# First unit's queries kept on the chip, and its maxima put ahead of the second block's keys

## The chip, the cores and the metric

One of the eight cores of one Trainium2 chip runs the kernel. The metric is the time of one execution in microseconds (us); the median of several runs is given. The engines named below are PE (TensorE, matrix products; PEld its weight loads), DVE (VectorE), ACT (ScalarE), POOL (GpSimd) and SP (SyncE, which issues most transfers).

## What is computed

A transformer block with modulated layer norms. There are 2048 rows of 512 numbers, 32 query heads of 16 numbers, and one key and value head that all of them share.

```python
mod = (silu(c) @ w_mod).reshape(1, 6, 1, -1)
sa, ca, ga, sb, cb, gb = (mod[:, i] for i in range(6))
h = layernorm(x) * (1 + ca) + sa
q = (h @ wq).reshape(1, 2048, 32, 16).transpose(0, 2, 1, 3)
k, v = h @ wk, h @ wv
p = softmax(einsum("bhqd,bkd->bhqk", q, k) * 16 ** -0.5)
o = einsum("bhqk,bkd->bhqd", p, v)
x = x + ga * (o.transpose(0, 2, 1, 3).reshape(1, 2048, 512) @ wo)
h = layernorm(x) * (1 + cb) + sb
x = x + gb * (gelu(h @ w1 + b1) @ w2 + b2)
```

## The kernel before

**Numbers in two parts.** Products run on rounded float32 (F32R). Each operand is split into a high part, which is the rounded number, and a low part, which is what the rounding left. A product of two such operands is three products summed in PSUM: high by high, low by high, high by low (`mm3`, with `split` to make the parts).

**Units.** The queries are cut into blocks of 256 rows, and each of those into 8 groups of 4 heads. One group of one block is a unit, 64 in all. A unit's queries lie in one of four buffers `qst` of 128 partitions. The partitions form two halves, s = 0 and s = 1, for the even and the odd pairs of heads. In each half, 16 rows hold the low part of the queries, 32 rows hold the high part twice, and rows 48 and 49 hold the unit's maxima (high and low part). The rows of `ks` that stand against them hold the keys' high part, high part, low part and -1. So one product of 64 rows gives the scores, and with the maxima in place it gives the scores less their maximum.

**Two passes over the keys.** For each unit the kernel first needs the maximum of every row of scores. `Max.step` issues one *max product* `m` (128 queries by 512 keys, line L517) on PE and one reduction `mx` on DVE (L522). The products use three PSUM banks, so the fourth product waits for the first reduction. When all 32 of a unit are done, `put_max` reduces once more, turns the result, and sends it by four small transfers into rows 48 and 49. Then `sexp` computes the score products `e` (L597), ACT takes the exponentials `p` (L598), and `pv` sums `acc` from them (L609). In the main loop, the e, p and acc of one unit run beside the max products of units further on and beside projections and the MLP, in an order that is fixed when the program is written.

**The prologue.** The change lies in the stretch before the main loop. Blocks there are 512 rows of `x`, four of them (0 to 3). For each block b: `stats1(b)` takes the row statistics on DVE; `xhat1(b)` normalises four tiles; `heads(b)` turns each of four column groups on PE (`turn1`, tiles `tp`) and applies the modulation (`mod1`, which makes the two parts of `h`); `keys(b)` sums keys and values (`kps`, 12 products in four steps) and `kv_out` copies them into `ks`; `low_k(b)` makes the keys' low part in half 0, and `repeat_k(b)` copies it into half 1.

Queries come from `qproj(b, g)`: 12 products sum the four pairs of heads of group g into one PSUM bank. The two parts are then sent to a tensor `dq` in DRAM (`send_q`), and `load_q(u)` fetches the rows of unit u back in the layout of `qst`: two transfers for each half, s = 1 first. Group 0 of block 0 serves units 0 and 1, group 1 serves unit 2.

All five engines run their instructions strictly in the order written (`manual_schedule`). `SLOTS` writes out the order of the last part of the prologue by hand. Each slot is a number of `Max.step`s, which alternate between the halves, followed by steps of other work named in the slot. `FIRST_MAX` is the order of the first 64 max products: pairs of unit and key block, eight products for each pair, four in each half. The key block `kc` needs `keys(kc)`, `low_k(kc)` and `repeat_k(kc)`. Before the main loop starts, 56 max products are issued: 54 in the slots and two in a loop behind them.

Ahead of the slots the order is: group 0 of block 0 is projected and sent while `stats1(2)` runs, and `load_q(0)` and `load_q(1)` follow; then `keys(0)`, `low_k(0)`, all of `heads(1)`, `stats1(3)`, `repeat_k(0)`, and `xhat1` of blocks 2 and 3 on ACT. The first slot has four max products and two steps of `keys 1`.

`prep_w2` belongs to the main loop. It loads 11 pieces of `w2`, multiplies them by a modulation row and splits them, on POOL; the last piece has 96 rows, and its tile is cleared first.

Of the kernel before, what the change touches and what calls it, by code (L numbers as in the profile page):

```python
# [14 lines left out]
P = 128  # L15
# [6 lines left out]
LEAD = 6  # L22
LEAD_0 = 6
FIRST_MAX = ((0, 0), (1, 0), (0, 1), (1, 1), (0, 2), (0, 3), (1, 2), (1, 3))
SLOTS = ((4, "keys 1", "keys 1"), (2, "keys 1", "keys 1"), (2, "low 1", "heads 2"), (2, "heads 2", "k 1"), (2, "heads 2"), (2, "heads 2", "v 0"),
# [4 lines left out]
MAX_WAIT = (1, 4)  # L30
# [17 lines left out]
def raw(ap):  # L48
    return ap.bitcast(F32)
# [3 lines left out]
def adaln_mqa_mlp(  # L53
# [76 lines left out]
    def split(dst_h, dst_l, src, eng_h, eng_l, between=None):  # L130
        if eng_h is nc.gpsimd:
            eng_h.tensor_scalar(out=dst_h, in0=src, scalar1=1.0, scalar2=0.0, op0=ALU.mult, op1=ALU.add)
        elif eng_h is nc.scalar:
            eng_h.copy(dst_h, src)
        else:
            eng_h.tensor_copy(out=dst_h, in_=src)
        if between:
            between()
        eng_l.tensor_tensor(out=dst_l, in0=src, in1=raw(dst_h), op=ALU.subtract)
# [188 lines left out]
    def prep_wq(g):  # L328
        gs = slice(g * P, (g + 1) * P)
        for j in range(2):  # L330
# [3 lines left out]
            nc.scalar.copy(dh, src)  # L334
            nc.gpsimd.tensor_tensor(out=dl, in0=src, in1=raw(dh), op=ALU.subtract)

    hts = {}
    hts_stats = {}
    pad(att, 64, "pad5")
# [13 lines left out]
            nc.gpsimd.tensor_scalar(out=nm, in0=nm, scalar1=-1.0, scalar2=0.0, op0=ALU.mult, op1=ALU.add)  # L353
        hts_stats[b] = mv, rs, nm

    def xhat1(b, eng):

        mv, rs, nm = hts_stats[b]
        xt = xts[b]
        for t in range(QT):  # L360
            if eng is nc.scalar:
                nc.scalar.activation(xt[:, t, :], xt[:, t, :], AF.Identity, scale=rs[:, t:t + 1], bias=nm[:, t:t + 1])
            else:
                eng.tensor_scalar(out=xt[:, t, :], in0=xt[:, t, :], scalar1=mv[:, t, 0:1], scalar2=rs[:, t:t + 1],
                                  op0=ALU.subtract, op1=ALU.mult)
            yield
# [15 lines left out]
    def kv_products(b):  # L382
        hH, hL = hts[b]
        kps[b] = psum.tile([P, BQ], F32, name=f"kps{b}", tag="x" if b == 3 else "v")
        return mm3(kps[b], [(wkH[:, k, :], wkL[:, k, :], hH[:, k, :], hL[:, k, :]) for k in range(KD)], 3)

    def kv_out(b):
        ps = kps[b]
        cols = slice(b * BQ, (b + 1) * BQ)
        vt = pro.tile([P, BQ], F32, name=f"vt{b}", tag="vt", bufs=2)  # L390
        for r in range(2):
            nc.scalar.copy(ks[64 * r:64 * r + 48, cols], ps[64 * r:64 * r + 48, :])
        nc.scalar.copy(vt[32:64, :], ps[32:64, :])
        vts[b] = vt

    def low_k(b):
        cols = slice(b * BQ, (b + 1) * BQ)
        nc.vector.tensor_tensor(out=ks[32:48, cols], in0=kps.pop(b)[32:48, :], in1=raw(ks[32:48, cols]), op=ALU.subtract)

    def repeat_k(b):  # L400
        cols = slice(b * BQ, (b + 1) * BQ)
# [727 lines left out]
    def prep_w2():  # L1129
        rp = wts_pool["rest"]  # L1130
        wfs = {}

        def load(f):
            fw = min(P, F - f * P)
            wf = wfs[f] = rp.tile([P, D], F32, name=f"w2f{f}", tag="wf", bufs=3)
            if fw < P:
                nc.gpsimd.memset(wf, 0.0)
            nc.sync.dma_start(out=wf[:fw], in_=w2[f * P:f * P + fw, :])

        def work(f):  # L1140
            g = f // KD
            if f % KD == 0:
                w2s.append([att.tile([P, min(KD, NF - f), D], F32R, name=f"w2{p_}{g}", tag=f"big{g + 1}{p_}") for p_ in "HL"])
            nc.gpsimd.tensor_tensor(out=wfs[f], in0=wfs[f], in1=gb, op=ALU.mult)
            split(w2s[g][0][:, f % KD, :], w2s[g][1][:, f % KD, :], wfs[f], nc.gpsimd, nc.gpsimd)

        for i, _ in enumerate(prepare(NF, load, work)):
            yield
            while i >= 1 and i - 1 < NF and not sent.issuperset(((i - 1) // KD + 1, g) for g in range(KD)):
                yield  # L1150
# [70 lines left out]
    def run(job, n=99):  # L1221
        for _ in range(n):
            if next(job, True):
                return
# [23 lines left out]
    def q_group():  # L1248
        for i in range(KD):
            next(projections[0])  # L1250
            if i == KD - 1:
                next(projections.pop(0))
            yield
# [5 lines left out]
    stats1(0)  # L1259
    run(xhat1(0, dve))  # L1260
    prep_wkv()
    prep_wq(0)
    for k in range(KD):
        mod_rows(psr, k, wms[k])
# [9 lines left out]
    load_constants()  # L1274
    mod1(0, 2, act, dve)
    mod1(0, 3, act, dve)
    rows = xhat1(1, act)
    run(rows, 2)

    def first_q(t):  # L1280
        if t == 1:
            run(q_group())
            load_q(0)
            load_q(1)

    stats1(2, first_q)
    run(rows)
    run(keys(0))
    low_k(0)
    load_mods(0)  # L1290
    load_mods(1)
    h1 = heads(1)
    run(h1, 2)

    def last_h(t):
        if t == QT - 1:
            run(h1)

    stats1(3, last_h)
    load_mods(2)  # L1300
    repeat_k(0)
    run(xhat1(2, act))
    run(xhat1(3, act))
    work = {"keys 1": keys(1), "heads 2": heads(2), "heads 3": heads(3), "q 1": q_group(), "keys 2": keys(2), "keys 3": keys(3),
# [198 lines left out]
```

## Time and profile before

| | us |
|---|---|
| median of 3 runs | 1586.05 |
| lowest and highest of them | 1585.31, 1586.48 |
| the profiled execution | 1589.15 |
| its span, first to last instruction | 1587.3 |

| engine | busy us | share of the span |
|---|---|---|
| PE | 1562.7 | 98% |
| DVE | 1406.0 | 89% |
| ACT | 1204.3 | 76% |
| POOL | 692.8 | 44% |

The profile is of one execution. An engine's share is a mean over stages with different limits, so it says little about one stage. A row of the timeline gives the start, the length, the engine, the line, the operation, the tiles written and read, the shape and the count. Brackets at its end hold how long the engine had been idle and what the profile takes to have ended the wait. Where a wait is for several things, the name is that of the one that came last by the profile's reckoning; if that had long been done, it was another, often a transfer. PEclk is the granted share of PE's full clock; the mean over the span is 0.992.

### The profile page before, as it was taken

The page shows a single profiled execution, that of the slowest core. Times are in us where ns is not written, and L with a number is a line of the kernel's source. Part 1 is how long each engine was busy: PE and PEld are TensorE (multiplying, and loading weights), DVE is VectorE, ACT ScalarE, POOL GpSimd, SP SyncE. Part 2 cuts the span into 40 slices and gives each one's busy share as a digit, 9 for nine tenths or more (in the row PEclk, how much of TensorE's full clock was granted, in tenths as well). Part 3 has the DMA queues.
Part 4 walks back from the last instruction along what each step waited for, and adds up shares of the span by engine and source line. Part 5 has one row for each costly group of instructions (what it writes and reads, how often), then busy time and mean ns, then how long its engine had stood idle before and what let it go on. Part 6 is the DMA issues. An engine that isn't in the chain of part 4 may idle for free.

```text
span 1587.3 us, 43409 instructions
## 1 busy us (share of the span) xinstructions
PE 1562.7 (98%) x17491; PEld 1043.9 (66%) x17491; DVE 1406.0 (89%) x2491; ACT 1204.3 (76%) x2417; POOL 692.8 (44%) x1242
## 2 busy tenths in 40 slices
PE   5999999999999999999999999999999999999999
PEld 3556655567766676666766676666766677676667
DVE  6889999899999998999999999999999999999715
ACT  5477777778877887778877887778877788778853
POOL 4345447446513472345622464334712465324721
PEclk8899999999999999999999999999999999999999
DMA  7135423312012120212112130212112130121231
GB/s 263 67 108 177 141 70 101 100 33 97 32 56 67 56 86 23 90 35 94 46 40 86 44 99 19 70 54 86 56 32 92 35 108 22 60 72 50 94 139 68
DMA packets 81022, 121.74 MB, mean 77 GB/s; under 512 B 15966, under 2 KB 55646, under 8 KB 80564
## 3 DMA queue, kind: packets, MB, share of 16 engines
q1 hardware_dynamic: 80804, 118.95, 22.6%
q8 instruction: 137, 2.24, 0.6%
q14 instruction: 65, 0.53, 0.1%
q10 hardware_dynamic: 16, 0.00, 0.0%
HBM read 91.13 MB, written 27.27 MB: 75 GB/s over the span
## 4 chain that ended last, share of the span: by engine, by line
PE 94%; ACT 3%; DVE 1%; DMA 1%; issue 0%; SPq 0%; POOL 0%; DVEq 0%; ACTq 0%
PE acc L609 32%; PE e L597 19%; PE m L517 19%; PE w1ps L193 8%; PE w2ps L193 6%; PE wops L193 3%; PE qps L193 2%; ACT p L598 2%; PE w2ps L187 2%; PE w1ps L187 1%; DVE mx L522 1%; PE tp L193 1%; PE kps L164 1%; PE tp L371 0%; PE modr L289 0%; DMA wm<-in_w_mod_dram 0%
## 5 line engine op out<-in xcount | busy, mean ns | idle before, releaser
L522 DVE TENSOR_REDUCE mx<-m 128x1 f32<-128x512 f32 x2048 | 1271.6, 681 | 105.6 <-PE m L517 95.6
L598 ACT ACTIVATE p<-e 128x512 f32<-128x512 f32 x2048 | 1066.6, 601 | 290.5 <-PE e L597 198.9
L517 PE MATMUL m<-ks,qst 64*128 64x512 f32 x2048 | 829.4, 433 | 6.4 <-DVE ve L205 4.9
L597 PE MATMUL e<-qst,ks 64*128 64x512 f32 x2048 | 729.5, 411 | 2.0 <-ACT wqH L334 1.3
L609 PE MATMUL acc<-p,va 128*32 128x256 f32 x8192 | 550.2, 385 | 1.7 <-DMA qst<-dq 1.7
L517 PEld LDWEIGHTS m<-ks,qst 64*128 64x128 f32 x2048 | 367.4, 184 | 104.6 <-DVE mx L522 85.7
L597 PEld LDWEIGHTS e<-qst,ks 64*128 64x128 f32 x2048 | 356.9, 184 | 112.6 <-ACT p L598 102.6
L609 PEld LDWEIGHTS acc<-p,va 128*32 128x32 f32 x8192 | 214.6, 109 | 219.6 <-issue 113.3
L193 PE MATMUL w1ps<-h2H,w1t 64*128 64x256 f32 x1232 | 236.6, 288 | 0.0
L193 PEld LDWEIGHTS w1ps<-h2H,w1t 64*128 64x128 f32 x1232 | 184.0, 185 | 31.7 <-issue 22.2
L566 POOL TENSOR_SCALAR mt<-turned 8x32 f32<-8x32 f32 x256 | 53.5, 209 | 342.7 <-DVE turned L572 330.6
L193 PE MATMUL w1ps<-h2L,w1t 64*128 64x256 f32 x616 | 169.5, 275 | 0.0
L193 PE MATMUL w2ps<-w2H,gH 64*128 64x256 f32 (+1 forms) x546 | 161.0, 295 | 0.0
L193 PE MATMUL w2ps<-w2H,gL 64*128 64x256 f32 (+1 forms) x546 | 153.9, 282 | 0.0
L193 PE MATMUL w2ps<-w2L,gH 64*128 64x256 f32 (+1 forms) x546 | 153.4, 281 | 0.0
L193 PEld LDWEIGHTS w1ps<-h2L,w1t 64*128 64x128 f32 x616 | 113.7, 185 | 0.0
L193 PEld LDWEIGHTS w2ps<-w2H,gH 64*128 64x128 f32 x546 | 100.5, 184 | 11.7 <-issue 5.4
L193 PEld LDWEIGHTS w2ps<-w2H,gL 64*128 64x128 f32 x546 | 100.7, 184 | 1.7
L193 PEld LDWEIGHTS w2ps<-w2L,gH 64*128 64x128 f32 x546 | 100.7, 184 | 1.3
L949 POOL TENSOR_SCALAR tt<-tt 128x256 f32<-128x256 f32 x77 | 31.2, 406 | 143.8 <-ACT tt L948 143.8
L193 PE MATMUL wops<-woH,onH 64*128 64x256 f32 x224 | 67.9, 303 | 0.0
L193 PE MATMUL wops<-woL,onH 64*128 64x256 f32 x224 | 62.2, 278 | 0.0
(220 smaller groups left out, 1613.1 us busy)
## 6 DMA issues: line engine op xcount, KB each, us to landing
w1t<-dw SPq DMA_DIRECT2D x82, 512.0 KB
qst<-dq SPq DMA_DIRECT2D x128, 64.0 KB
do<-oc SPq DMA_DIRECT2D x64, 128.0 KB
dw<-w1s SPq DMA_DIRECT2D x11, 512.0 KB
xt<-in_A_x_dram SPq DMA_DIRECT2D x4, 1024.0 KB
dq<-qH SPq DMA_DIRECT2D x16, 256.0 KB
dq<-qL SPq DMA_DIRECT2D x16, 256.0 KB
qst<-dq SPq DMA_DIRECT2D x128, 32.0 KB
```

Source lines behind the costliest of these rows:

```text
L164: nc.tensor.matmul(ps, a, b_, start=begin and n == 0, stop=end and n == last)
L187: nc.tensor.matmul(ps, a, b_, start=first_, stop=last_)
L193: nc.tensor.matmul(ps, a[rows], b_[rows], start=first_ and s == 0, stop=last_ and s == 1)
L517: nc.tensor.matmul(m, qsts[u][rows, j, t * P:(t + 1) * P], ks[rows, kc * 512:(kc + 1) * 512], start=True, stop=True)
L522: nc.vector.tensor_reduce(out=self.mx[u][:, i, kc:kc + 1], in_=m, axis=AX.X, op=ALU.max)
L566: nc.gpsimd.tensor_scalar(out=mt[:, g:g + 32], in0=turned[g:g + 4 * T, :], scalar1=1.0, scalar2=0.0, op0=ALU.mult, op1=ALU.add)
L597: nc.tensor.matmul(e, ks[rows, kt * P:(kt + 1) * P], rhs, start=True, stop=True)
L598: nc.scalar.activation(ptiles[u, K][:, j, s, :], e, AF.Exp, scale=0.25)
L609: ins = nc.tensor.matmul(accs[u][32 * cidx:32 * cidx + 32, :], va[:, kt, :], rhs, start=kt == 0, stop=kt == NKT - 1)
L949: nc.gpsimd.tensor_scalar(out=tt, in0=tt, scalar1=1.0, scalar2=1.0, op0=ALU.mult, op1=ALU.add)
```

## The change

Four edits.

1. A second set of weights `w0H`, `w0L` holds the 64 columns of `wq` that unit 0 needs, each head's 16 columns repeated three times in the layout of `qst`. `prep_w0` makes it on ACT and POOL ahead of `prep_wq(0)`. `first_products` sums unit 0's queries with them, right into the rows of a PSUM tile that match `qst`, beside the keys of block 0. `first_queries` copies them to `qst` and subtracts in place for the low rows. Unit 0's queries don't go through DRAM any more. The keys' low part of block 0 is made for both halves on DVE (`low_keys`).
2. The eight max products of unit 0 on key block 0 now stand in pairs between the four steps of `heads(1)`, ahead of the slots. Group 0's projection, which unit 1 still needs, and `load_q(1)` stand between them too. `stats1(3)` follows them.
3. `SLOTS` has eight fewer max products, so that all is one group of eight ahead and exactly 56 are issued before the main loop.
4. Two of block 1's four tiles are normalised on POOL, and `prep_w2` clears the 32 missing rows of the last piece's two parts rather than the whole tile that it loads.

```diff
-SLOTS = ((4, "keys 1", "keys 1"), (2, "keys 1", "keys 1"), (2, "low 1", "heads 2"), ...
-         (2, "heads 3"), ..., (0, "keys 2"), (2, "keys 2"), (2, "keys 2"), (2, "keys 2"),
-         (2, "low 2", "k 2", "v 1", "wq 1"), (0, "keys 3"), (2, "keys 3"), ...
+SLOTS = ((2, "keys 1", "keys 1"), (2, "keys 1", "keys 1"), (2, "low 1", "heads 2"), ...
+         (2, "heads 3"), ..., (0, "keys 2"), (1, "keys 2"), (1, "keys 2"), (1, "keys 2"),
+         (1, "low 2", "k 2", "v 1", "wq 1"), (0, "keys 3"), (2, "keys 3"), ...
...
+    def prep_w0():
+        for j in range(2):
+            for s in range(2):
+                at = 32 * s + 16 * j
+                w = wqf[:, :, at:at + 16].unsqueeze(2).to_broadcast([P, KD, 3, 16])
+                dh, dl = (t[:, :, j, 64 * s:64 * s + 48].rearrange("p k (o r) -> p k o r", r=16) for t in (w0H, w0L))
+                nc.scalar.copy(dh, w)
+                nc.gpsimd.tensor_tensor(out=dl, in0=w, in1=raw(dh), op=ALU.subtract)
...
+    def first_products(k):
+        if k == 0:
+            kps[0] = psum.tile([P, BQ], F32, name="kps0", tag="v")
+            kps["q"] = psum.tile([P, 2, HQ], F32, name="q0ps", tag="x")
+        hH, hL = hts[0]
+        for n, (w, h) in enumerate(((w0H, hH), (w0L, hH), (w0H, hL))):
+            for j in range(2):
+                nc.tensor.matmul(kps["q"][:, j, :], w[:, k, j, :], h[:, k, 0:HQ], start=k + n + j == 0,
+                                 stop=k == KD - 1 and n + j == 3)
+        for n, (w, h) in enumerate(((wkH, hH), (wkL, hH), (wkH, hL))):
+            nc.tensor.matmul(kps[0], w[:, k, :], h[:, k, :], start=k + n == 0, stop=k == KD - 1 and n == 2)
+
+    def first_queries():
+        ps = kps.pop("q")
+        qsts[0] = qbufs[0]
+        nc.scalar.copy(qbufs[0], ps)
+        for s in range(2):
+            rows = slice(64 * s, 64 * s + 16)
+            nc.vector.tensor_tensor(out=qbufs[0][rows], in0=ps[rows], in1=raw(qbufs[0][rows]), op=ALU.subtract)
...
+    def low_keys(s):
+        nc.vector.tensor_tensor(out=ks[64 * s + 32:64 * s + 48, 0:BQ], in0=kps[0][64 * s + 32:64 * s + 48, :],
+                                in1=raw(ks[64 * s + 32:64 * s + 48, 0:BQ]), op=ALU.subtract)
...
-            if fw < P:
-                nc.gpsimd.memset(wf, 0.0)
...
+            if fw < P:
+                for t in w2s[g]:
+                    nc.gpsimd.memset(raw(t[fw:, f % KD, :]), 0.0)
...
     prep_wkv()
+    prep_w0()
     prep_wq(0)
...
-    rows = xhat1(1, act)
-    run(rows, 2)
-
-    def first_q(t):
-        if t == 1:
-            run(q_group())
-            load_q(0)
-            load_q(1)
-
-    stats1(2, first_q)
-    run(rows)
-    run(keys(0))
-    low_k(0)
+    run(xhat1(1, act, range(2)))
+    run(xhat1(1, pool, range(2, QT)))
+    for k in range(KD):
+        first_products(k)
+    stats1(2, lambda t: first_queries() if t == 1 else None)
+    kv_out(0)
+    low_keys(0)
+    low_keys(1)
+    kps.pop(0)
     load_mods(0)
     load_mods(1)
     h1 = heads(1)
-    run(h1, 2)
-
-    def last_h(t):
-        if t == QT - 1:
-            run(h1)
-
-    stats1(3, last_h)
+    q0 = q_group()
+    run(h1, 1)
+    chunk(2)
+    run(h1, 1)
+    run(q0, 2)
+    chunk(2)
+    run(h1, 1)
+    run(q0)
+    chunk(2)
+    run(h1, 1)
+    load_q(1)
+    chunk(2)
+    stats1(3)
     load_mods(2)
-    repeat_k(0)
     run(xhat1(2, act))
     run(xhat1(3, act))
```

More of the change, by code (lines that the diff above doesn't have):

```diff
@@ L24 @@
 FIRST_MAX = ((0, 0), (1, 0), (0, 1), (1, 1), (0, 2), (0, 3), (1, 2), (1, 3))
-SLOTS = ((4, "keys 1", "keys 1"), (2, "keys 1", "keys 1"), (2, "low 1", "heads 2"), (2, "heads 2", "k 1"), (2, "heads 2"), (2, "heads 2", "v 0"),
[2 rows of a table removed]
+SLOTS = ((2, "keys 1", "keys 1"), (2, "keys 1", "keys 1"), (2, "low 1", "heads 2"), (2, "heads 2", "k 1"), (2, "heads 2"), (2, "heads 2", "v 0"),
[2 rows of a table added]
          (0, "v 2"), (2, "q 1"), (2, "q 1"), (2, "q 1"),
@@ L335, in prep_wq @@
             nc.gpsimd.tensor_tensor(out=dl, in0=src, in1=raw(dh), op=ALU.subtract)
+    w0H = pro.tile([P, KD, 2, P], F32R, name="w0H")
+    w0L = pro.tile([P, KD, 2, P], F32R, name="w0L")
+    for w0 in (w0H, w0L):
+        for s in range(2):
+            nc.gpsimd.memset(raw(w0[:, :, :, 64 * s + 48:64 * s + 64]), 0.0)
+    def prep_w0():
[6 more added lines that the diff above has]
+                nc.gpsimd.tensor_tensor(out=dl, in0=w, in1=raw(dh), op=ALU.subtract)
     hts = {}
@@ L354, in stats1, with xhat1 @@
         hts_stats[b] = mv, rs, nm
-    def xhat1(b, eng):
+    def xhat1(b, eng, tiles=range(QT)):
         mv, rs, nm = hts_stats[b]
         xt = xts[b]
-        for t in range(QT):
+        for t in tiles:
             if eng is nc.scalar:
@@ L385, in kv_products @@
         return mm3(kps[b], [(wkH[:, k, :], wkL[:, k, :], hH[:, k, :], hL[:, k, :]) for k in range(KD)], 3)
+    def first_products(k):
[13 more added lines that the diff above has]
+        nc.scalar.copy(qbufs[0], ps)
+        for s in range(2):
+            rows = slice(64 * s, 64 * s + 16)
+            nc.vector.tensor_tensor(out=qbufs[0][rows], in0=ps[rows], in1=raw(qbufs[0][rows]), op=ALU.subtract)
     def kv_out(b):
@@ L1143, in work @@
                 w2s.append([att.tile([P, min(KD, NF - f), D], F32R, name=f"w2{p_}{g}", tag=f"big{g + 1}{p_}") for p_ in "HL"])
-            nc.gpsimd.tensor_tensor(out=wfs[f], in0=wfs[f], in1=gb, op=ALU.mult)
-            split(w2s[g][0][:, f % KD, :], w2s[g][1][:, f % KD, :], wfs[f], nc.gpsimd, nc.gpsimd)
+            fw = min(P, F - f * P)
+            nc.gpsimd.tensor_tensor(out=wfs[f][:fw], in0=wfs[f][:fw], in1=gb[:fw], op=ALU.mult)
+            split(w2s[g][0][:fw, f % KD, :], w2s[g][1][:fw, f % KD, :], wfs[f][:fw], nc.gpsimd, nc.gpsimd)
+            if fw < P:
+                for t in w2s[g]:
+                    nc.gpsimd.memset(raw(t[fw:, f % KD, :]), 0.0)
         for i, _ in enumerate(prepare(NF, load, work)):
```

4 rows, old and new, of the table SLOTS are left out of this document.

## The prediction

> **What bounds the kernel now.** I read the page's engine shares and its chain first, then stretches of the span, then the order of instructions in the stretch that the diff touches. Two lines of the page, then two stretches (columns: length; PE, PEld, DVE, ACT, POOL busy us and count; granted TensorE clock; DMA share and GB/s):
>
> ```profile
> PE 1562.7 (98%) x17491; PEld 1043.9 (66%) x17491; DVE 1406.0 (89%) x2491; ACT 1204.3 (76%) x2417; POOL 692.8 (44%) x1242
> PE 94%; ACT 3%; DVE 1%; DMA 1%; issue 0%; SPq 0%; POOL 0%; DVEq 0%; ACTq 0%
> ...
> 0.00:82.69 82.69, 64.47 (x264) 34.07 (x265) 62.02 (x120) 44.40 (x75) 35.55 (x63) 0.88 0.46 159
> 82.69:1560.00 1477.31, 1474.71 (x17095) 989.90 (x17096) 1328.19 (x2328) 1150.47 (x2319) 657.25 (x1180) 1.00 0.22 73
> ```
>
> From 82.69, where the first score product e starts, PE is busy 1474.71 of 1477.31 us at full clock. That order of work is the same after the change, 56 max products are issued ahead of it in both kernels, so what the diff does to the time is what it does to the moment of the first e. Slack lies only before it: PE 64.47 of 82.69, clock 0.88. The next rows are that stretch in order of time (start, length, engine, line, what; idle before and releaser), with the stretches of the max products alone (L517) between them:
>
> ```profile
> 24.00 0.69 DVE L438 TENSOR_TENSOR qL<-qps,qH 128x512 fp32r<-128x512 f32 x1 [0.92 <-ACT qH L437]
> 24.72 0.34 SPq L415 DMA_DIRECT2D dq<-qL  x1
> 26.74 0.69 SPq L487 DMA_DIRECT2D qst<-dq  x1
> 28.94 0.65 SPq L488 DMA_DIRECT2D qst<-dq  x1
> 33.45 1.19 PE L517 MATMUL m<-ks,qst 64*128 64x512 f32 x3 [4.90 <-DVE ve L205]
> ...
> 33.45:42.47 9.02, 3.27 (x9) 1.23 (x9) 0.61 0.94 349
> 42.47:82.69 40.22, 16.49 (x48) 6.40 (x48) 0.87 0.12 43
> ...
> 82.69 0.62 PE L597 MATMUL e<-qst,ks 64*128 64x512 f32 x2 [1.34 <-ACT wqH L334]
> ```
>
> The queries of units 0 and 1 go out to DRAM and come back: qL ends at 24.69, unit 0's last load is issued at 28.94, the first max product runs at 33.45. The releaser named, a statistic of another block, isn't read by that product; the load is. So I read 33.45 - 24.69 = 8.76 us as the price of the round trip. Unit 1's first product, the ninth, is at 42.47, with 48 up to the first e.
>
> **The change part by part.**
>
> *Weights w0.* Four 128x192 casts on ACT and four subtractions on POOL stand ahead of prep_wq(0).
>
> ```profile
> 10.02 1.04 POOL L207 TENSOR_TENSOR rs<-ve,mhalf 128x4 f32<-128x4 f32 x1 [3.64 <-DVE ve L205]
> 13.45 0.75 ACT L334 CAST wqH<-wqf 128x256 fp32r<-128x256 f32 x2 [10.17 <-DMA wqf<-in_A_wq_dram]
> 13.96 1.55 POOL L335 TENSOR_TENSOR wqL<-wqf,wqH 128x256 fp32r<-128x256 f32 x2 [2.90 <-ACT wqH L334]
> 14.65 0.58 ACT L299 COPY modr_sb<-modr 64x512 f32<-64x512 f32 x1 [0.46 <-PE modr L289]
> 17.90 1.29 POOL L139 TENSOR_TENSOR h0L<-h,h0H 128x512 fp32r<-128x512 f32 x1 [2.39 <-ACT h0H L134]
> ```
>
> A cast costs at most 0.38 (half of 0.75), 0.28 by width; four cost 1.1, ACT had 0.46 to spare before modr_sb, on which all of h0 hangs: +0.7 us (0 to 1.05). POOL's four, at most 0.78 each, fill its 2.39 idle; without that cover they would add about 0.7. The four small clears of w0 fall into POOL's 3.64 idle before 10 us; uncovered they would cost less than 1.
>
> *First products.* 24 query products of 256 columns replace 12 of 512; the 12 key products stay. The stretch of the old 24 (line L164 alone: PE and PEld busy), and one group of their weight loads (count, busy, mean ns, idle before):
>
> ```profile
> 18.40:25.25 6.85, 6.49 (x24) 4.29 (x24) 1.00 0.89 276
> ...
> L164 PEld LDWEIGHTS qps<-h0L,wqH 128*128 128x128 f32 x4 | 0.7, 187 | 1.1 <-DVE h0L L139 0.4 <-POOL h0L L139 0.4
> ```
>
> A 256-column product costs between half of 6.49/24 (0.14) and its weight load (0.19); I take 0.19, since each has a load of its own: 24 x 0.19 against 12 x 0.27, +1.3, less up to 1.1 in which PE waited for h0L anyway. With the 0.7, keys end near 26.4 instead of 25.25, the queries near 25.7.
>
> *The first maxima, earlier.* No send, no load for unit 0. Instead one ACT copy, two subtractions of 16 partitions on DVE in the middle of the statistics, and a second low-part subtraction instead of ACT's repeat.
>
> ```profile
> 23.40 0.56 ACT L437 CAST qH<-qps 128x512 fp32r<-128x512 f32 x1
> 24.60 1.28 DVE L199 BATCH_NORM_STATS2 st<-xt 128x6 f32<-128x512 f32 x2
> 25.80 0.36 DVE L203 BATCH_NORM_AGGREGATE mv<-st 128x2 f32<-128x6 f32 x4
> 27.07 0.68 DVE L398 TENSOR_TENSOR ks<-kps,ks 16x512 fp32r<-16x512 f32 x1 [0.71 <-ACT vt L393]
> ```
>
> Copy to 26.3, two subtractions 1.4, two statistics 1.28, aggregation and variance 0.6, keys' low part 0.68: the first product at 30.6 (29.9 to 31.5), its partner 0.6 later. That is 2.8 us sooner, if PE then had something to follow with.
>
> *Unit 1's queries, later.* This is where I see the loss. Group 0's projection, which unit 1 needs, now stands on PE behind the first two products: product pair, transposes, six projections, pair, transposes, six more, and only then qH, qL, send, load. The ninth product stands on PE ahead of all of keys 1. Rows for the pieces, at the half clock first (stretches, then rows), then at the full one:
>
> ```profile
> 26.64:33.45 6.81, 0.66 (x4) 0.45 (x5) 5.34 (x12) 6.64 (x11) 4.90 (x6) 0.77 0.17 48
> 30.60:40.40 9.80, 6.59 (x15) 3.80 (x16) 5.59 (x13) 7.55 (x11) 3.15 (x4) 0.50 0.78 274
> 47.30:57.50 10.20, 10.20 (x35) 6.02 (x33) 6.53 (x11) 6.63 (x11) 8.94 (x8) 0.50 0.30 104
> ...
> 35.71 0.79 PE L164 MATMUL kps<-big1H,wkH 128*128 128x512 f32 x1
> 38.57 0.79 PE L517 MATMUL m<-ks,qst 64*128 64x512 f32 x2
> 39.29 0.79 PE L164 MATMUL kps<-big1H,wkH 128*128 128x512 f32 x1
> 41.45 0.50 PE L517 MATMUL m<-ks,qst 64*128 64x512 f32 x2
> 48.10 1.11 PE L371 MATMUL tp<-ident,xt 128*128 128x128 f32 x4
> ...
> 64.39 0.50 PE L164 MATMUL kps<-big3H,wkH 128*128 128x512 f32 x1
> 65.28 0.51 PE L517 MATMUL m<-ks,qst 64*128 64x512 f32 x2
> 65.72 0.51 PE L164 MATMUL kps<-big3H,wkH 128*128 128x512 f32 x1
> ```
>
> After 6 us with 0.66 of PE work the clock was 0.50 for 9.8 us. The change leaves PE as idle from 27 to 30.6, so I take the same. At half clock six projections cost 38.57 - 35.71 = 2.86, a pair 0.72, transposes 1.1; the partner product ends at 31.6, and 31.6 + 1.1 + 2.86 + 0.72 + 1.1 + 2.86 = 40.2. At full clock (three projections 0.89, a pair 0.44, transposes half of 1.1) it is 31.4 + 0.55 + 1.78 + 0.44 + 0.55 + 1.78 = 36.5. I take 39.0, nearer to the half-clock row. Then qH 0.56 and qL 0.69 with their waits, 1.4, and the trip 8.76: the ninth product at 49.2, instead of 42.47: **+6.7**. Bounds: full clock 46.7; half 50.4; and if something else than the load had set 33.45, a trip of at least 4.9 (to the last issue's end, 29.59), 45.3: +2.8 to +7.9. The first maxima's 2.8 us are in this already; they buy nothing else. What waits behind that product on PE is keys 1, and with it everything; xhat of blocks 2 and 3 on ACT and the fourth block's statistics on DVE run meanwhile, hidden by it.
>
> [...]
>
> *Keys 1 behind it.* Before, its 12 products lay ahead of 42.47: 35.71 to 41.45 less a pair of 0.72, 5.0 us. After, they lie behind 49.2 and on PE's path. PE comes to them from an idle stretch, as before, so **+5.0** (4 x 0.89 = 3.6 at full clock, 2 x 2.86 = 5.7 at half).
>
> *Slots.* One chunk of eight is ahead, so blocks 2's and 3's keys are wanted one slot sooner after they are made.
>
> ```profile
> 60.21 0.39 PE L164 MATMUL kps<-big2L,wkH 128*128 128x512 f32 x1
> 63.15 0.62 ACT L402 CAST ks<-ks 16x512 fp32r<-16x512 f32 x1 [0.75 <-DVE ks L398]
> 63.55 0.18 PEld L517 LDWEIGHTS m<-ks,qst 64*128 64x128 f32 x1 [0.37 <-DVE ks L398]
> ```
>
> From the last key product to the first that reads them are 2.95 us, and PE already waits 0.37. A slot less of cover is 0.89 + 0.44 = 1.33 for each of two blocks; I take **+2.2** (0 to 2.7).
>
> *The end of the stretch.* Unit 0's maxima are sent one slot sooner, so the 1.34 idle before e goes. But ACT issues two of the sends, and the copies of "q 1" now stand behind them:
>
> ```profile
> 74.19 0.59 ACT L441 COPY q<-qps 128x512 f32<-128x512 f32 x1 [4.10 <-PE qps L164]
> 78.90 1.50 ACTq L561 DMA_DIRECT2D qst<-mh  x1
> 80.50 0.58 ACTq L561 DMA_DIRECT2D qst<-ml  x1
> ```
>
> That delays the first exponentials by some 0.8, and unit 2's send and load too, on SP behind the maxima: **-0.5** (-1.34 to +2).
>
> *At nothing:* two tiles of xhat1(1) on POOL instead of ACT, hidden by the products of block 0 (uncovered at most two of the 1.29 above); load_mods issued sooner on SP, since two sends and eight loads no longer stand ahead of it, and its rows are needed last of all; w2's clears on POOL, 44% busy (one of 128x512 gone, two of 32 partitions added, uncovered within one 1.29).
>
> Sum: 6.7 + 5.0 + 2.2 - 0.5 = +13.4. The profiled execution took 1589.15 for its span of 1587.3, so 1602.5; the runs' median, 1586.05, lies 3.1 below it, so **1599**.
>
> **The rivals.** *The clock stays full.* The products that now start at 30.6 keep PE busy enough. Then the ninth product is at 46.7 (+4.2), keys 1 costs 3.6, slots and end 1.7, and the loss of the 10.2 us at 0.50 from 47.30 (half, 5.1) is saved: +4.4, 1590. Against it: PE is idle both before 30.6 and before the ninth product, and the row from 47.30 shows half clock with PE busy throughout. [...]
>
> *Faster.* DVE, not PE, paces the stretch: the trip lies under the reductions and the fourth block's statistics, and keys 1 fits into PE's gaps. Then the earlier start and the vanished idle stand alone, -2.8 - 1.34 = -4.1, 1582. By my sum it decides only where the ninth product comes sooner than 42.47 by all that follows it (5.0 + 2.2 - 0.5), at 35.8, qL thus by 27.0; but qL's projection stands behind a product at 30.6. DVE busy 62.02 of 82.69 speaks against it too.
>
> *No change:* smaller trip and smaller clock loss together cancel the rest, 1586.
>
> *Worse.* The half clock also covers keys 2 and 3, whose slots hold one product less, or unit 2's load comes late: +5 more, 1604.
>
> **How the numbers follow.** The forecast gets 0.55 (its own range 1593 to 1603), the full clock 0.15, worse 0.18, faster 0.06, no change 0.06. 0.2% is 3.2 us, about what can be told from no change. Some 0.04 of the full clock falls within it: faster 0.06, same 0.10, slower 0.84. Low: the trip's and the clock's lower bounds, 13.4 - 3.9 - 5.1 = 4.4, with part of the no-change case, 1589. High: the upper bounds (+1.2, +0.7, +0.5, +2.5) and 5 make 23, not all at once: 1608.
>
> **What would show it.** Right: first max product near 30.6; a PE idle stretch of 6 to 10 us ending at the ninth, released by a load of qst, near 49; keys 1 behind it; waits of over 1 us at the first products on keys 2 and 3; the first e near 96 with no idle before it; the rest as before. Wrong: the ninth product before 43, or a clock of 1.00 from 30 to 60, or a later stretch that takes the loss back.

## The result, and the profile after

The changed kernel takes 1606.14 us (median of 4 runs, 1605.62 to 1607.47) beside 1586.26 for the kernel before on the same chip: ratio 1.0122, 95% interval 1.0105 to 1.0140. It is slower by some 20 us. The forecast was 1599 in a range from 1589 to 1608, so sign and place were right and the size was 7 us short. By the spans of the two profiled executions, which the sum was made of, the loss is 18.3 us where +13.4 was forecast; the other 2 us come from the step to the median, which lies 1.3 below the profiled execution here and 3.1 below it before. Even that is less agreement than it looks like, since two errors of opposite sign stand behind it: the prologue lost more than forecast, and a part that was costed at nothing won 3 us elsewhere.

First the page of the kernel after (engine shares, chain), then stretches of it up to the first score product e, from there, and from the ninth max product to it (columns as in the prediction):

```profile
PE 1571.6 (98%) x17515; PEld 1048.8 (65%) x17515; DVE 1405.7 (88%) x2494; ACT 1203.2 (75%) x2419; POOL 700.0 (44%) x1253
...
PE 94%; ACT 3%; DVE 1%; DMA 1%; issue 0%; SPq 0%; POOL 0%; DVEq 0%; POOLq 0%; ACTq 0%
...
0.00:104.16 104.16, 76.45 (x288) 41.22 (x289) 61.70 (x123) 43.30 (x74) 40.39 (x71) 0.79 0.36 119
104.16:1578.00 1473.84, 1471.27 (x17096) 987.30 (x17093) 1327.92 (x2328) 1150.16 (x2321) 659.60 (x1183) 1.00 0.23 73
48.84:104.16 55.32, 50.52 (x176) 25.73 (x177) 33.25 (x53) 19.82 (x37) 15.06 (x22) 0.73 0.06 21
```

The page as a whole hardly differs from that of before. The loss is all in the first row: it has grown from 82.69 to 104.16 us, its clock has sunk from 0.88 to 0.79, and PE's busy time has grown by 12 us. The 24 more records in it are the first unit's own query products, which account for 2.8 us of that (below). The other 9.2 are near what the clock gives: PE was busy for 35.9 us at half clock before the first e, 17.0 in the kernel before, and a pair of max products with the three query products behind it took 2.30 us at 0.50 (from 93.98) and 1.33 at 1.00 (from 96.28). By that the 18.9 us more at half clock cost an estimated 8.0. The main loop is no longer than before: from the first e to the last it takes 1446.6 us, before 1449.7.

The timeline of that stretch in the kernel after, with the products that mark the forecast's steps (max products are L559 here, e is L639), and the end of the projection with its send and last load:

```profile
29.14 1.58 PE L559 MATMUL m<-ks,qst 64*128 64x512 f32 x2 [1.95 <-DVE ks L439]
...
37.70 0.68 DVE L480 TENSOR_TENSOR qL<-qps,qH 128x512 fp32r<-128x512 f32 x1
38.41 0.33 SPq L457 DMA_DIRECT2D dq<-qL  x1
42.64 0.64 SPq L530 DMA_DIRECT2D qst<-dq  x1
48.84 0.89 PE L559 MATMUL m<-ks,qst 64*128 64x512 f32 x2 [9.31 <-DMA qst<-dq]
...
58.38 0.50 PE L559 MATMUL m<-ks,qst 64*128 64x512 f32 x1 [0.28 <-DVE ks L436]
60.43 0.50 PE L559 MATMUL m<-ks,qst 64*128 64x512 f32 x1 [1.56 <-ACT ks L444]
...
78.58 0.49 PE L559 MATMUL m<-ks,qst 64*128 64x512 f32 x1 [0.88 <-DVE ks L436]
79.23 0.79 PE L559 MATMUL m<-ks,qst 64*128 64x512 f32 x1 [0.16 <-ACT ks L444]
88.73 0.50 PE L559 MATMUL m<-ks,qst 64*128 64x512 f32 x1 [1.78 <-DVE ks L436]
...
104.16 0.50 PE L639 MATMUL e<-qst,ks 64*128 64x512 f32 x2
105.67 0.50 PE L559 MATMUL m<-ks,qst 64*128 64x512 f32 x2 [1.01 <-ACT modl_sb L1365]
```

The first max product comes 4.3 us sooner than before, and the ninth 6.4 later, after an idle stretch of 9.31 that ends with unit 1's load. Then the products on the keys of blocks 1, 2 and 3 wait in turn. The third thing is the clock. These are the half-clock stretches from the wait for the ninth product on:

```profile
41.60:55.30 13.70, 6.46 (x15) 4.20 (x16) 5.18 (x13) 3.62 (x5) 1.40 (x3) 0.50 0.29 91
62.10:72.30 10.20, 10.20 (x36) 5.98 (x34) 6.33 (x10) 7.24 (x12) 7.46 (x8) 0.50 0.31 104
79.20:86.00 6.80, 6.77 (x14) 3.34 (x14) 3.87 (x6) 0.94 (x3) 1.64 (x5) 0.50 0.01 2
89.40:96.20 6.80, 6.80 (x14) 3.32 (x14) 3.83 (x6) 0.17 (x1) 0.00 (x0) 0.50 0.00 0
```

From 48.84 on that is 6.5 + 10.2 + 6.8 + 6.8 = 30.3 us at half clock, where the kernel before had 10.2 behind its ninth product. In the last three rows PE is busy all but 0.03 us and the clock is at half all the same. Each of these three stretches begins within 2 us of a wait for keys (1.56 at 60.43, 0.88 at 78.58, 1.78 at 88.73), and none of these waits is as long as 2 us. The last two stretches hold key, query and max products only, no transposes.

### The profile page after: what moved, and what is told of

Read it like the earlier page. It is cut to its first block, busy times and chain, and to the rows that moved or that the text cites. A ratio compares the mean times of both kernels' runs of the same rounds, so it can differ in the third digit from the quotient of the medians.

```text
span 1605.6 us, 43467 instructions
## 1 busy us (share of the span) xinstructions
PE 1571.6 (98%) x17515; PEld 1048.8 (65%) x17515; DVE 1405.7 (88%) x2494; ACT 1203.2 (75%) x2419; POOL 700.0 (44%) x1253
## 4 chain that ended last, share of the span: by engine, by line
PE 94%; ACT 3%; DVE 1%; DMA 1%; issue 0%; SPq 0%; POOL 0%; DVEq 0%; POOLq 0%; ACTq 0%
PE acc L651 31%; PE e L639 19%; PE m L559 18%; PE w1ps L193 8%; PE w2ps L193 6%; PE wops L193 3%; PE qps L193 2%; ACT p L640 2%; PE w2ps L187 2%; PE w1ps L187 1%; PE tp L193 1%; PE kps L164 1%; DVE mx L564 1%; DMA qst<-dq 1%; PE tp L387 1%
## 5 line engine op out<-in xcount | busy, mean ns | idle before, releaser
L559 PE MATMUL m<-ks,qst 64*128 64x512 f32 x2048 | 832.7, 434 | 18.6 <-DMA qst<-dq 9.9
L639 PE MATMUL e<-qst,ks 64*128 64x512 f32 x2048 | 727.7, 411 | 0.7
L559 PEld LDWEIGHTS m<-ks,qst 64*128 64x128 f32 x2048 | 368.0, 185 | 119.8 <-DVE mx L564 86.3
L639 PEld LDWEIGHTS e<-qst,ks 64*128 64x128 f32 x2048 | 356.5, 184 | 110.9 <-ACT p L640 102.9
L193 PEld LDWEIGHTS w1ps<-h2H,w1t 64*128 64x128 f32 x1232 | 183.9, 184 | 31.7 <-issue 22.6
```

The source lines that it names most:

```text
L193: nc.tensor.matmul(ps, a[rows], b_[rows], start=first_ and s == 0, stop=last_ and s == 1)
L559: nc.tensor.matmul(m, qsts[u][rows, j, t * P:(t + 1) * P], ks[rows, kc * 512:(kc + 1) * 512], start=True, stop=True)
L639: nc.tensor.matmul(e, ks[rows, kt * P:(kt + 1) * P], rhs, start=True, stop=True)
```

## The experiments

Three causes were to be told apart: the late trip of unit 1's queries, the order of keys and slots, and the clock. To hold the clock, dead products ("fills", 128 rows by 512 columns, whose result nothing reads) were added to PE's work. The table gives for each kernel the start of the first and the ninth max product and of the first e in its trace, the time at half clock between 28 us and that e, the median, and the ratio to the runs of before made beside it on the same chip (their medians: 1587.27 for e1 to e4, 1586.15 for e5 to e8, 1587.08 for e9 to e11, 1585.51 for e12).

| kernel | first m | ninth m | first e | at half | median us | ratio (95%) |
|---|---|---|---|---|---|---|
| before | 33.45 | 42.47 | 82.69 | 20.5 | 1586.26 | |
| after | 29.14 | 48.84 | 104.16 | 44.4 | 1606.14 | 1.0122 (1.0105-1.0140) |
| e1, group 0 first | 31.89 | 39.63 | 100.72 | 54.6 | 1601.52 | 1.0084 (1.0062-1.0105) |
| e2, keys 1 first | 29.04 | 47.81 | 95.43 | 30.7 | 1602.71 | 1.0099 (1.0081-1.0117) |
| e3, after, fill in groups of one | 29.26 | 72.37 | 120.94 | 44.4 | 1628.37 | 1.0259 (1.0242-1.0276) |
| e4, before, 8 fills | 33.40 | 42.50 | 82.15 | 17.1 | 1587.30 | 1.0000 (0.9990-1.0009) |
| e5, after, filled | 28.90 | 46.30 | 97.97 | 20.5 | 1599.99 | 1.0083 (1.0062-1.0104) |
| e6, order of before | 31.48 | 46.76 | 83.12 | 10.2 | 1585.68 | 0.9997 (0.9985-1.0008) |
| e7, e6 filled | 31.65 | 47.46 | 86.05 | 10.2 | 1587.32 | 1.0006 (0.9996-1.0015) |
| e8, before, 16 fills | 33.40 | 42.60 | 81.08 | 10.2 | 1587.28 | 1.0001 (0.9992-1.0011) |
| e9, no waits, filled | 31.86 | 41.37 | 90.32 | 13.7 | 1594.61 | 1.0047 (1.0032-1.0062) |
| e10, e9 unfilled | 31.69 | 40.94 | 87.59 | 20.5 | 1592.91 | 1.0038 (1.0025-1.0051) |
| e11, w2 part alone | 33.94 | 43.10 | 81.88 | 17.1 | 1582.09 | 0.9969 (0.9957-0.9981) |
| e12, w2 part and 38 fills | 32.54 | 39.55 | 78.05 | 0 | 1582.41 | 0.9982 (0.9973-0.9991) |

The first four columns are of one execution each, and executions of one kernel differ by several us. In most kernels the time goes with the clock granted over the whole execution: in e1 from 1597.60 at 0.990 to 1604.00 at 0.983 (the last is the profiled one), in e2 from 1600.01 at 0.990 (profiled) to 1605.25 at 0.984, in e10 from 1587.31 at 0.996 to 1596.58 at 0.988 (profiled: 1589.16 at 0.993). So the order of instructions alone does not fix how long the clock is at half, and a trace can show more or less of it than the median has.

**e1: the trip taken off the path.** Edit to the changed kernel:

```diff
     kv_out(0)
+    run(q_group())
+    load_q(1)
     low_keys(0)
...
-    run(q0, 2) ... run(q0) ... load_q(1)    # from between the maxima
```

> The changed kernel with one thing moved back: group 0's whole projection, its send and load_q(1) stand ahead of unit 0's first maxima again (right behind kv_out(0)); nothing else differs. Late-trip theory (the loss is unit 1's round trip, which starts behind the first maxima): the ninth max product comes near 40.5 us instead of 48.84 (projection done by 29.5, qL near 30.8, trip about 10), the wait ahead of it falls from 9.3 to under 3 us, first e near 95 instead of 104, median 1596 to 1599, which leaves 10 to 12 us of the 20. Clock theory (the loss is half clock in later stretches, whatever started it): the ninth product moves as above but the time by under 3 us where the same later stretches stay at half clock. Slot theory (keys wanted one slot too soon): the waits at the first products on blocks 1, 2 and 3 stay, 1.8, 1.0 and 1.8 us.

The ninth product came at 39.63 without a wait, 9.2 us sooner than after. Of that the first e kept 3.4 and the median 4.6. What took the rest back is the stretch from the ninth product to the first e, 61.1 us long against 55.3:

```profile
53.00:80.30 27.30, 26.97 (x72) 14.82 (x72) 13.31 (x21) 11.44 (x20) 12.04 (x15) 0.50 0.12 40
```

The trace is of the longest of the four executions; the others were granted more clock (0.985 to 0.990 against 0.983), so this half clock is not all due to the order. The ninth product came as the late-trip theory had it; first e near 95 and 1596 to 1599 did not. The waits at the keys of blocks 1 and 3 stayed (1.71 and 1.78), as the slot theory had it; the one at block 2's went. So the trip is a cause, but its price can't be read off the wait that it ends: the clock moved with it.

**e2: keys 1 ahead of unit 1's maxima.**

```diff
-SLOTS = ((2, "keys 1", "keys 1"), (2, "keys 1", "keys 1"), (2, "low 1", "heads 2"),
+SLOTS = ((0, "keys 1", "keys 1"), (0, "keys 1", "keys 1"), (6, "low 1", "heads 2"),
```

> The changed kernel with the four steps of keys 1 put ahead of unit 1's first max product; the four max products of the first two slots follow them in the third slot. Late-trip theory: the ninth product still comes near 48.8 us, but keys 1 (5.35 us of PE behind it in the changed kernel) lies under the wait, so first e comes 4 to 6 us sooner, median 1600 to 1602. Clock theory: PE is then busy through most of the wait, the stretch at half clock from 41.6 becomes shorter, and 2 to 3 us more are won. If the wait were not what holds PE: no change.

PE's wait shrank from 9.31 to 4.83 with keys 1 in it, and the first e came 8.7 us sooner than after. The median is 3.4 lower; the profiled execution (1600.01) was the fastest of its runs. The ninth product to the first e took 47.6, still 7.4 more than before, of which 19.1 at half clock behind the ninth (before: 10.2) account for some 4 (an estimate by the same 1.33 for 2.30) and the waits at keys, 3.8 in all, for much of the rest. The 8.7 are what the late-trip theory (4 to 6) and the clock theory (2 to 3 more) give together; the median lies just above the 1600 to 1602 of the late-trip theory alone.

**e3: a first filling of the wait.** Forty dead products ahead of slot 0, each a group of its own in one PSUM bank, and one ahead of most slots.

```diff
+    fill(40, "x")      # 40 x matmul(ps_i, ..., start=True, stop=True), all in one bank
     for i, (n, *names) in enumerate(SLOTS):
+        if 2 <= i < 24 and i not in (10, 15, 20):
+            fill(1, "v" if 15 < i < 20 else "x")
```

> The changed kernel with products added whose results nobody reads: 40 of 512 columns in the wait ahead of unit 1's first max product, and one ahead of each slot from the third to the 24th (not the ones without a max product). They hold PE busy and change no other order. Clock theory: the granted clock stays at or near 1.00 from 42 on, the 30 us that were at half clock behind the ninth product (half, 15 us) come back less about 19 x 0.23 = 4.4 us for the added ones, so first e near 93, median 1594 to 1598. Late-trip theory alone: the ninth product stays near 48.8, only keys 1 gets cheaper by 1.7, the added products cost up to 4, median 1604 to 1610.

Both theories missed, since the filling itself cost the time. Fills that are each a group of their own started 0.56 us apart at full clock and 0.85 apart at half (from 41.98 on), and forty held the ninth product back to 72.37:

```profile
39.63 4.65 PE L289 MATMUL fill<-wkH 128*128 128x512 f32 x7
```

So the time says nothing on the clock. The stretch behind the ninth product shrank to 48.6 us from 55.3, but that doesn't single out the clock either: the other engines had 23 us more to make the keys ready, and the waits for keys are gone.

**e5: the same with one group.** `fill(30)` as one accumulation group, one ahead of slots 2 to 9, three ahead of slots 10 and 14:

```diff
+        for i in range(n):
+            nc.tensor.matmul(ps, wkH[:, 0, :], ..., start=i == 0, stop=i == n - 1)
```

> The changed kernel with 30 dead products (full rows, 512 columns, one group) in TensorE's wait ahead of the ninth max product, one more ahead of each of slots 2 to 9 and three ahead of slots 10 and 14; their result is read by nothing. Unlike the fill before, they are one group, so that none of them waits. Theory 'half clock behind the ninth product costs 7 us': the ninth product stays within 1 us of 48.8 (the load sets it), the 55.3 us from it to the first score product fall to 47 to 50, time 1598 to 1601. Rival 'the slots' waits for keys set that stretch, the clock only goes along with them': the stretch stays within 2 us of 55.3, time 1604 to 1608.

```profile
38.59 7.11 PE L290 MATMUL fill<-wkH 128*128 128x512 f32 x30
46.30 0.59 PE L566 MATMUL m<-ks,qst 64*128 64x512 f32 x2 [0.59 <-DMA qst<-dq]
...
46.30:97.97 51.67, 47.96 (x191) 25.20 (x191) 33.17 (x53) 22.17 (x41) 15.70 (x22) 0.83 0.08 29
57.20:67.40 10.20, 10.20 (x36) 6.28 (x35) 6.05 (x10) 5.59 (x10) 6.50 (x6) 0.50 0.32 105
84.50:91.30 6.80, 6.80 (x16) 3.34 (x15) 3.86 (x6) 0.00 (x0) 0.00 (x0) 0.50 0.00 0
```

Thirty dead products took 7.11 us at full clock, 0.24 each. The clock stayed full through the wait and through keys 1, and of the other stretches two remained: half clock behind the ninth product fell from 30.3 to 17.1 us. The time fell by 6.1, to 1599.99. The stretch is 51.7 long, 3.6 less than after and between the two theories' 47 to 50 and 53 to 57. In this trace 2.5 us more come from a ninth product at 46.3, where 48.8 was expected, behind a first stretch at half clock of 3.4 instead of 6.8 us; that one lies ahead of every fill, so it is not their doing. The 44 fills only add work and moved nothing else, and every one of the four times lies below all those of the kernel after. The half clock is thus a cause by itself: more PE work gave less time. The two remaining stretches begin some 2 us behind waits of 1.38 and 1.78 (the 18th and the 41st max product); behind the wait at the 33rd, now 0.24 instead of 0.88, there is none. That such waits set the half clock off isn't shown: in the kernel before a stretch begins at 47.4 without one.

**e6: the order of before.** The direct queries, the POOL tiles and the w2 part stay; group 0 and `load_q(1)` come right behind `kv_out(0)`, all of `heads(1)` ahead of the maxima, and `SLOTS` is that of before.

```diff
-SLOTS = ...    # as after
+SLOTS = ...    # as before
...
+    run(q_group())
+    load_q(1)
     load_mods(0)
     load_mods(1)
-    h1 = heads(1) ... chunk(2)    # the maxima between the head rows
+    run(heads(1))
     stats1(3)
```

> The direct queries alone: the first unit's queries summed in the rows that the max products read, but group 0's products and unit 1's load right behind, then the head rows of block 1, and the maxima in the slots of the kernel before (block 1's keys among the first unit's maxima). Theory 'the loss is in the order, not in the direct queries': first max product 32 to 34, ninth without a wait of over 1 us at 41 to 43, first score product 81 to 85, time 1584 to 1589. Rival 'the late trip stays': ninth at 45 or later, released by the load, time 1590 or more. Rival 'clock': no such wait, but over 25 us at half clock between 28 and 95 us and the first score product behind 88, time 1592 to 1598.

First e 83.12 and 1585.68, as the first theory had it, and the time of before. So nearly all of the 20 us hang on the order, not on how the first unit's queries are made. But the sooner queries also win nothing:

```profile
39.39 0.79 PE L559 MATMUL m<-ks,qst 64*128 64x512 f32 x1 [7.18 <-DVE mx L564]
...
34.50:44.70 10.20, 5.31 (x11) 3.22 (x12) 7.15 (x16) 6.08 (x9) 2.24 (x4) 0.50 0.81 294
46.76:83.12 36.36, 34.18 (x161) 17.11 (x161) 33.26 (x55) 19.58 (x38) 16.58 (x24) 1.00 0.13 45
```

Three max products run from 31.48, then PE waits 7.18, because the reductions stand on DVE behind the low parts of block 1's rows and `stats1(3)`. The ninth is at 46.76 (forecast 41 to 43, missed; no load is waited for). From there on DVE is busy 33.26 of 36.36 at full clock. Since e6 holds the w2 part too, it has to be compared with e11, not with before: by the ratios (0.9997 and 0.9969) the rest of the edit costs some 4 us even in this order.

**e4, e7, e8: filling where the clock sinks without the change.** Dead products ahead of slots 2 to 9 of the kernel before (e4), and 16 in 14 of the slots 2 to 19 of e6 (e7) and of before (e8).

> The kernel before with one such added product ahead of each of the eight slots of heads 2 and heads 3. Clock theory: the stretch at half clock from 47.4 to 57.6 goes or shrinks, the slots are paced by DVE (1.31 us) rather than by PE at half clock (1.77), first e 3 to 4 us sooner, median 1582 to 1584. If the half clock costs nothing there (DVE hides it): eight products of 0.23 more, median 1586 to 1588.

```profile
47.40:57.60 10.20, 10.20 (x49) 5.70 (x49) 9.16 (x15) 6.31 (x11) 8.37 (x8) 1.00 0.32 104
67.00:73.80 6.80, 6.80 (x18) 3.26 (x21) 3.85 (x7) 0.44 (x1) 0.00 (x0) 0.50 0.01 2
```

The stretch that was at 0.50 is at 1.00, and a new one behind it is at 0.50: won and given back. The time, 1587.30, is the one forecast for a half clock that costs nothing, though for another reason.

> The direct queries alone, and single dead products ahead of 14 of the slots 2 to 19 (one or two each) to hold the clock. Clock theory: 3 to 8 us less at half clock before the first score product than in the direct queries alone, and as much earlier first score product, 79 to 82, time 1580 to 1586. Rival 'other waits set it': the time of the direct queries alone, within 1.5 us.

> The kernel before with the same dead products ahead of slots 2 to 19 (the earlier try had eight, in slots 2 to 9, and won 3.4 us that a new half-clock stretch at 67.0 to 73.8 gave back). Clock theory: that stretch is gone too, the first score product at 78 to 80 instead of 82.7, time 1582 to 1584. Rival 'that gain is taken back by what the end of the prologue waits for': first score product near 82, time 1586 to 1588.

e7 missed: e6 had no half clock there to win, so 16 products at 0.24 only added; first e 2.9 later. In e8 half clock between 40 us and the first e is gone and e came 1.6 sooner, yet the time stayed, as the rival had it. Where that went is told under e11.

**e9, e10: group 0 first, the keys' lead restored.** As e1, with one max product less in each of the first two slots; e9 with `fill(3)` behind each head row and `fill(6)` ahead of slot 0, e10 without.

```diff
-SLOTS = ((2, "keys 1", "keys 1"), (2, "keys 1", "keys 1"), ...
+SLOTS = ((1, "keys 1", "keys 1"), (1, "keys 1", "keys 1"), ...
+        fill(3)    # e9 only, behind each of the four head rows
+    fill(6)        # e9 only, ahead of slot 0
```

> The changed kernel with group 0's products and unit 1's load ahead of the maxima (as in the first order), one max product instead of two ahead of each of the first two slots (so that the keys of blocks 1 to 3 have as much lead as in the kernel before), and three dead products behind each of block 1's four head rows and six ahead of slot 0, to hold the clock. Theory 'the loss is three things, the load's trip, the slots and the clock, each of them in the order': ninth max product 38 to 41 without a wait of over 1 us, at most 15 us at half clock between 28 and 95 us, no wait of over 1 us at block 2's and 3's keys, first score product 77 to 82, time 1580 to 1586. Rival 'maxima ahead of block 1's keys cost by themselves, since VectorE has no more of them to do behind': first score product behind 86, time over 1590.

> The same without the dead products. Theory: more than 25 us at half clock between 28 and 95 us, first score product 6 us or more behind that of the filled one, time 1588 to 1598. Rival 'the clock goes along, it doesn't set': within 2 us of the filled one.

Both theories missed, and the figures of both rivals came. The ninth product came at 41 and the waits of over 1 us at keys 2 and 3 are gone, as expected, yet the first e came only at 90.32 and 87.59. In the traces a step stands out that the change moved and that the expectations left out, `stats1(3)`. In e9:

```profile
45.15 2.93 ACT L384 ACTIVATE xt<-xt,nm,rs 128x512 f32<-128x512 f32 x4 [3.64 <-POOL nm L375]
47.98 1.17 ACT L436 CAST ks<-kps 48x512 fp32r<-48x512 f32 x2
...
51.23 0.53 PE L565 MATMUL m<-ks,qst 64*128 64x512 f32 x1 [3.07 <-DVE mx L570]
```

The statistics of block 3 now follow eight reductions on DVE; ACT waits 3.64 us for them with xhat of block 3, and the copies of block 1's keys, whose last product starts at 45.04, stand behind that on ACT until 47.98. On DVE the keys' low part waits for these copies, the next reductions stand behind it, and PE waits 3.07 for one of them. The seventeenth product, the first to read those keys, is at 52.74 (e9) and 52.04 (e10), 49.15 before. An earlier ninth product buys little while block 1's keys don't come sooner. These 3.6 and 2.9 us are about half of the 7.6 and 4.9 by which the first e lies behind that of before. They are read from two traces; no run moves `stats1(3)` alone.

e10 is no slower than e9, so the dead products won nothing in this order. That doesn't clear the clock: e9 was at half for 13.7 us from 51.6 on all the same, behind the wait of 3.07, and e10's own twelve times go with the clock, as said above.

**e11: the part on w2 alone**, in the kernel before.

```diff
-            if fw < P:
-                nc.gpsimd.memset(wf, 0.0)          # in load(f), ahead of the transfer
...
-            nc.gpsimd.tensor_tensor(out=wfs[f], in0=wfs[f], in1=gb, op=ALU.mult)
+            fw = min(P, F - f * P)                  # in work(f), behind it
+            nc.gpsimd.tensor_tensor(out=wfs[f][:fw], in0=wfs[f][:fw], in1=gb[:fw], op=ALU.mult)
...
+            if fw < P:
+                for t in w2s[g]:
+                    nc.gpsimd.memset(raw(t[fw:, f % KD, :]), 0.0)
```

> The kernel before with the part on w2's last piece alone: no clearing of the loaded piece, work on its filled rows only, and two clears of the tails. Prediction's term: nothing, within 0.2% of the kernel before, 1585 to 1588. Rival: the two clears on POOL hold up something in the second half of the span, more than 1 us slower.

The multiplication and the split of the last piece work on its 96 filled rows alone, which belongs to the change as well. Neither theory: the kernel is faster than before by 0.3% (0.19 to 0.43%), the only clear gain of the whole change. The queue of SP and the two engines around it, in the kernel before (waits of SP's queue: us, times, longest; then the timeline):

```profile
SPq L1138 <- POOL w2f L1137: 4.9, 1, 4.9
...
281.13 0.54 POOL L1137 MEMSET w2f<- 128x512 f32 x1
281.69 0.34 SPq L1138 DMA_DIRECT2D w2f<-in_B_w_dram  x1
286.23 0.61 SPq L487 DMA_DIRECT2D qst<-dq  x1
289.45 0.45 SPq L490 DMA_DIRECT2D qst<-dz  x1
...
289.00 0.62 PE L609 MATMUL acc<-p,va 128*32 128x256 f32 x2 [0.85 <-DMA qst<-dq]
290.44 1.24 PE L609 MATMUL acc<-p,va 128*32 128x256 f32 x12 [0.82 <-DMA qst<-dq]
```

And in e11:

```profile
SPq L1136 <- POOL w2L L139: 1.1, 1, 1.1
...
276.31 0.34 SPq L1136 DMA_DIRECT2D w2f<-in_B_w_dram  x1
280.96 0.61 SPq L487 DMA_DIRECT2D qst<-dq  x1
284.19 0.45 SPq L490 DMA_DIRECT2D qst<-dz  x1
```

The clearing costs POOL 0.54 us. But it stands on POOL behind two pieces' work, SP's load of the piece waits 4.9 us for it, and behind that load on SP stands the load of a unit's queries, which PE then waits for. The distance between the 1105th and the 1169th acc product, on both sides of it, is 13.52 us in before, 13.27 in e4 and 15.31 in e8, which clear the loaded piece, and 10.43 to 10.69 in the eleven others, which don't: 3.1 us, and in e8 4.9. There PE had come 2.5 us sooner to the same load and lost 1.8 more at it; this is where most of the filling's gain went. (An `acc` product reads no `qst`; the profile infers the name. But in e11 that load is issued 5.3 us sooner, with PE itself only 1.6 sooner, and PE shows no such wait.) The median of e11 is 4.9 us lower, more than the 3.1; in the trace most of the rest lies about the first e, ahead of the edit, where the clock differs (6.8 us at half behind the ninth product, 10.2 before).

**e12: both.** e8's fills, 4 ahead of block 1's head rows and 18 ahead of the first max product, with the w2 part.

> The kernel before with the part on w2's last piece and with dead products: 4 ahead of block 1's first head rows, 18 ahead of the first max product, where TensorE waits 4.9 us, and those of the second filling of the kernel before in slots 2 to 19. Theory 'the two gains are of different places and add': no half clock between 30 and 82 us, first max product still near 33.5 (its keys' rows set it), the nine us from it to the ninth shortened by 1 to 3, first score product 77 to 81, no wait of the score step for unit loads near 290 us, time 1577 to 1582. Rival 'the clock's gain is given back again': the time of the part on w2 alone, 1581 to 1584. Rival 'the dead products delay what they stand ahead of': over 1584.

```profile
0.00:78.05 78.05, 64.89 (x302) 36.28 (x303) 62.29 (x120) 44.09 (x75) 35.59 (x63) 1.00 0.51 169
78.05:1552.00 1473.95, 1473.05 (x17095) 988.82 (x17096) 1328.44 (x2329) 1150.57 (x2318) 656.86 (x1181) 1.00 0.23 73
```

By the trace the gains add: no half clock before the first e, which comes at 78.05, and no wait near 290; this execution took 1581.21. By the medians they don't: 1582.41 here, 1582.09 in e11, and the two intervals overlap; this is what the rival "given back again" had. The clock was held in all eleven executions (0.999 or more, 0.994 to 0.997 in e11), so it isn't that. Single executions of one kernel lie up to 5 us apart (the kernel before, beside e11: 1584.33 to 1589.46), more than what is in question, and one execution of each was profiled. That holding the clock with 38 dead products is worth anything on top of the w2 part is not shown. The w2 part alone beats both kernels.

## Why the prediction was right, and where it was not

*Trip, +6.7.* Measured +6.4 (48.84 for 49.2), with the idle stretch and the releaser that it named. Two errors in it cancel, so that it came this close is luck. The projection was done sooner (qL ends at 38.38, forecast 40.4), because PE got from half to full clock in the middle of it (0.50 from 28.0 to 34.8, 1.00 from there to 41.6), and the trip from there took 10.5 us rather than the 8.76 read off the first unit.

*Keys 1, +5.0.* From 49.66 to 55.74, less one pair: 5.4, at half clock (0.50 up to 55.3) as assumed.

*Slots, +2.2.* Mis-sized. The waits at block 2's and 3's keys came as told, 0.88 + 0.16 and 1.78. The step left out block 1, whose keys had been two slots ahead and were now wanted as soon as they were made: 0.28 + 1.56. Together 4.7; PE shows no wait at these products before.

*End, -0.5.* The idle 1.34 before e is gone. A wait of 1.01 behind it and smaller ones bring the shift from 21.5 at the first e to 22.6 at the ninth, so -0.25 in all.

*The clock behind the ninth product, nothing.* This is the step that failed by most. The sum tacitly kept before's one stretch of 10.2 us. There were 30.3, of which 6.5 lie under keys 1 and are counted there. Half of the other 23.8 is 11.9, against 5.1 before: +6.8, an estimate, since it takes all of that time to be PE's and half of it to be the clock's; by the 1.33 for 2.30 of the profile after it is 5.7. The prediction had it as the rival "worse", at 5 us and a chance of 0.18, and e5 shows that this part is real: with 13.3 us less at half clock and 14 dead products more (3.3 us) the stretch is 3.6 shorter, about half of 13.3 again. The stretch at 0.50 from 47.30 in the kernel before holds transposes; those from 79.2 and 89.4 here, at 0.50 too, hold none.

With these sizes, 6.4 + 5.4 + 4.7 - 0.25 + 6.8 = 23.0 (22.0 with the 5.7), for 22.6 measured at the ninth e. The terms are not independent, since the clock moves with the waits (e1, e5).

*w2's clears, nothing.* Wrong, by -3.1. The prediction looked at POOL's own share and not at which queue waits for the instruction: SP's load, and behind that a unit's load. The trace of before showed both (the wait of 4.9 and PE's waits at 289.00 and 290.44). Less this and 1.2 us of small differences, the 22.6 become the 18.3 by which the two spans differ.

*First products.* The weights `w0` cost the 0.7 forecast: the last transposes ahead of these products start at 17.91 instead of 17.22. The 0.19 for a query product of 256 columns was too much; two of them start every 0.23:

```profile
22.34 0.39 PE L411 MATMUL q0ps<-h0H,w0H 128*128 128x256 f32 x2
22.57 0.39 PE L411 MATMUL q0ps<-h0H,w0L 128*128 128x256 f32 x2
```

So 24 take 2.8 us, queries ended at 24.6 instead of 25.7, and the first maximum came at 29.14 instead of 30.6. It was told rightly that this buys nothing. xhat on POOL was put at no more than 1.29 a tile and took 2.07, so the first head row of block 1 waited 1.30 us on PE; it is off the path of the first max product, which DVE's low keys release after 1.95 us of idle.

*The rival "clock full"* fell by the four stretches at 0.50. *The rival "faster, DVE paces"* fell as predicted, since the ninth product came 13 us behind the 35.8 from which it would have decided. e6 and e9 show waits for DVE (7.18 and 3.07) as soon as the load is out of the way.

## What to carry to other kernels

Work that is put ahead of its old place leaves a hole where it stood: here eight max products had covered the trip of the next queries and filled the half-empty slots, and without them PE waited 9.31 us for the load, and ran at half clock for 44.4 us between 28 us and the first e instead of 20.5. Cost a removed instruction by what waits for it on other queues, not by its own length: a clearing of 0.54 us held SP for 4.9 and PE for 3.1. And where a stretch runs below full clock, a sum of waits and durations at a fixed clock is no forecast (30.3 us at half clock behind the ninth product, where the sum kept 10.2); take the clock stretch by stretch as an unknown, with both ends in the range.

## What was not expected of the hardware

In the kernel after, half clock came and went in stretches of 6.8, 10.2 and 13.7 us, three of the four shown with PE busy for all but 0.03 us. From 62.10 to 72.30 PE was busy 10.20 of 10.20 us at 0.50, and no wait between the ninth product and the first e was longer than 1.78. In e4 eight dead products of 128 rows, 2 us of work spread over the 10 from 40.9, went with a clock of 1.00 from 47.40 to 57.60, where the kernel before had 0.50 beside the same transposes and max products of 64 rows; e8 and e12, filled the same way there, kept 1.00 too.

At full clock, dead products that are each a group of their own in one bank started 0.56 us apart (e3, 39.63 to 41.86, five of them), those in one group 0.24 (e5, 30 in 7.11).
